# Linear attention and an ELU feed-forward on one core: K and V of four batches on all 128 rows, one chunk moved up, the last copy split

## The chip, the cores and the metric

The kernel runs on one core of one Trainium2 chip. The metric is device time in microseconds of that core, as the median of several executions of the whole program. The engines named below are PE (TensorE, matmuls, with its weight loads), DVE (VectorE), ACT (ScalarE), POOL (GpSimd, which here also issues the loads) and SP (SyncE, which issues transposing transfers and stores). PSUM is the memory that PE writes its sums to.

## The reference

Eight batches with eight heads of 576 rows and 64 columns go through linear attention, a norm per head, and a feed-forward with an ELU between two matrices of 512 x 2048 and 2048 x 512.

```python
kv = np.einsum('bhsd,bhse->bhde', k, v)
out = np.einsum('bhsd,bhde->bhse', q, kv)
rms = np.sqrt(np.mean(out * out, axis=-1, keepdims=True) + 1e-06)
x = out / rms * g_norm            # then heads side by side: 4608 tokens of 512
h = x @ w_in
g = np.where(h > 0.0, h, np.exp(np.minimum(h, 0.0)) - 1.0)
return g @ w_out
```

## The kernel before

A tile is 512 tokens, so there are nine tiles (`NT`) over eight batches. One tile is cut from rows that lie 64 to a group: a head's 576 rows are 64 groups of nine consecutive rows (`RK` = 9), and a matmul takes one row of each group.

**K and V.** `load` (L88) lays a batch of K or V into a tile `[128, 4, 9, 64]`: partition and index m together run through the heads, so that two heads lie on the two halves of the partitions, and each partition holds nine rows of a head in one piece of 2304 bytes of float32, which the DMA turns to bfloat16. `kv_mm` (L151) makes K^T V of the eight heads: for each of nine rows, two partition halves `s`, and two column halves `l`, for two values of `u`, one matmul of 64 rows x 64 columns with 64 elements; 72 in a batch. The four quarters of the array are taken in turn. The sums go to `kv_sb` (L268 by ACT, for batches 2 to 7).

**Order.** The order of work is written out by hand (a manual schedule); only waits and buffers are placed by the framework. Each engine works through its own list in order. Batch 0 is made in four chunks of two heads, L577 to L652: `chunk_kv` (K^T V), `chunk_kv_out` (its copy by DVE), `chunk_y` (q times it), `chunk_square` (ACT), `mean_mm` (the mean over a head by a matmul with a constant matrix), a logarithm and an exponential on ACT for one over the root, `chunk_scale` (DVE), and `early` (the products with `w_in` for the first three pairs of blocks, chunk by chunk). `idle` (L523) issues matmuls with zeros that fill waiting time. After that PE alternates products of the first matrix (`mm1`, L390, 32 groups of four for a tile), of the second (`mm2`, L399) and pieces of the next tile's attention. From tile 2 on that is `window` (L753), in which `kv` of batch T + 1 stands behind the first pair of blocks of tile T.

**Loads.** They are issued by POOL in the order of the program. For batches 2 to 7 `fetch_ahead` (L92) issues q, K and V; `cast_q` (L98) rearranges q on POOL after that; `turn_q` (L328) turns it by DMA on SP; and `after_turn` (L336) holds POOL until q is turned, before the next batch is fetched. The tiles of K and V come from a pool with three buffers each. Software DMAs share eight semaphores in turn, so a DMA also waits for the one eight before it.

**End.** The last tile's last 128 tokens are made in two halves of 256 columns by `last_columns` (L434): 16 matmuls, then a copy from PSUM (ACT for the first half, DVE for the second, L448), then `last_store` (L423), one store on ACT's queue and one on SP's.

Of the kernel before, what the change touches and what calls it, by code (L numbers as in the profile page):

```python
# [9 lines left out]
BF16 = mybir.dt.bfloat16  # L10
# [6 lines left out]
def kernel(  # L17
# [13 lines left out]
    nc = tc.nc  # L31
    P = 128

    B, H, S, D = q.shape
    DM = H * D
    DF = moe_w_in.shape[1]
    RK = S // 64
    J = 4
# [3 lines left out]
    NT = B + 1  # L42
    V, A, Q = nc.vector, nc.scalar, nc.gpsimd
# [3 lines left out]
    qkvp = ctx.enter_context(tc.tile_pool(name="qkvp", bufs=3))  # L47
# [27 lines left out]
    def slot_of(T, n):  # L75
        return divmod(8 * T + n, RK)

    bf, raw = {}, {}
    src_of = {"q": q, "k": k, "v": v}

    def fetch(name, b, u=None):

        if (name, b) not in bf:
            bf[name, b] = qkvp.tile([P, 4, RK, D], BF16, name=f"{name}_bf", tag=name)
        ms = slice(0, 4) if u is None else slice(u, 4, 2)
        load(bf[name, b][:, ms], name, b, ms)

# [4 lines left out]
    def fetch_ahead(b):  # L92
        raw[b] = stage.tile([P, 4, RK, D], FP32, name="st_q", tag="q")
        load(raw[b], "q", b)
        for name in "kv":
            fetch(name, b)

    def cast_q(b):  # L98

# [8 lines left out]
    def copy_on(eng, out_, in_):  # L108
        if eng is nc.scalar:
            nc.scalar.copy(out_, in_)  # L110
        else:
            eng.tensor_copy(out=out_, in_=in_)  # L112
# [16 lines left out]
    def single(tag, name):  # L129
        pool = ps_x if tag == "x" else ps_m2  # L130
        return pool.tile([P, 512], FP32, name=name, tag=tag)

    def pair(tag, name):
        if tag in ("x", "m", "mx"):
            return [single(t, name) for t in (tag + tag)[:2]]
        return ps_m1.tile([P, 2, 512], FP32, name=name, tag=tag)
# [14 lines left out]
    def kv_mm(b, kv_ps, u, ls=range(2)):  # L151
        for j in range(RK):
            for s in range(2):
                rows = slice(s * 64, s * 64 + 64)
                for l in ls:
                    nc.tensor.matmul(  # L156
                        kv_ps[s][l * 64 : l * 64 + 64, u * 64 : u * 64 + 64],
                        lhsT=bf["k", b][rows, 2 * l + u, j, :],
                        rhs=bf["v", b][rows, 2 * l + u, j, :],
                        start=(j == 0),  # L160
                        stop=(j == RK - 1),
                    )

    def kv_out(b, kv_ps, u, engs):
        for s in range(2):
# [92 lines left out]
    def attention(T):  # L258

        st = {}  # L260

        def kv():
            if T == B:
                return
            kv_ps = at_tile()
            for u in range(2):
                kv_mm(T, [kv_ps[:, s, :] for s in range(2)], u)
            nc.scalar.copy(  # L268
                kv_sb[:, T], kv_ps[:, :, 0:P].rearrange("p s (u e) -> p u s e", u=2)
            )  # L270

        def se(h):
            def product():
                st["se", h] = at_tile()
                se_mm(T, h, st["se", h])
                sq = attp.tile([P, 2, DM], BF16, name="sq", tag="sq")
                nc.scalar.activation(sq, st["se", h], AF.Square)  # L277
                st["sq", h] = sq

            def sums():  # L280
                ss = attp.tile([P, 2 * H], FP32, name="ss", tag="ss")
                st["ss", h] = ss
                nc.vector.reduce_sum(  # L283
                    out=ss,
                    in_=st.pop(("sq", h)).rearrange("p l (m e) -> p (l m) e", e=D),
                    axis=AX.X,
                )

            def inv():
                ss = st["ss", h]  # L290
                nc.scalar.activation(ss, ss, AF.Ln, bias=eps_col, scale=1.0 / D)
                nc.scalar.activation(ss, ss, AF.Exp, scale=-0.5)  # L292

            def scale():
                if h == 0:
                    st["xs"] = attp.tile([P, J, DM], BF16, name="xs", tag="xs")
                    x_tile(T)
                se_ps, ss = st.pop(("se", h)), st.pop(("ss", h))
                nc.vector.tensor_tensor(  # L299
                    out=st["xs"][:, 2 * h : 2 * h + 2, :].rearrange("p i (l m e) -> p l i m e", l=2, e=D),  # L300
                    in0=se_ps.rearrange("p l (i m e) -> p l i m e", i=2, e=D),
                    in1=ss.rearrange("p (l i m) -> p l i m", l=2, i=2).unsqueeze(4).to_broadcast([P, 2, 2, 4, D]),
                    op=ALU.mult,
                )
                for i in (2 * h, 2 * h + 1):
                    nc.sync.dma_start_transpose(
                        out=xT[T][:, :, i * P : i * P + P], in_=st["xs"][:, i, :]
                    )

            def gain():  # L310
                cols = slice(2 * h * P, 2 * h * P + 2 * P)
                nc.vector.tensor_scalar(  # L312
                    out=xT[T][:, :, cols],
                    in0=xT[T][:, :, cols],
                    scalar1=g_col,
                    scalar2=None,
                    op0=ALU.mult,
                )

            return product, sums, inv, scale, gain  # L320

        pieces = {"kv": kv}
        for h in range(2):
            for name, piece in zip(("se", "sum", "inv", "mul", "gain"), se(h)):
                pieces[f"{name}{h}"] = piece
        return pieces
# [96 lines left out]
    def last_store(j, o, cols):  # L423
        rows = out_dram.rearrange("(b p j) f -> b p j f", b=B, j=RK)
        for h, eng in enumerate((nc.scalar, nc.sync)):
            b, jj = slot_of(NT - 1, 2 * j + h)
            eng.dma_start(out=rows[b][:, jj, cols], in_=o[h * 64 : h * 64 + 64])
# [5 lines left out]

    def last_columns():  # L434

        for n, eng in enumerate((A, V)):
            cols = slice(n * 256, n * 256 + 256)
            ps = single("m", "o_ps")[:, 0:256]
            for f in range(FC):
                nc.tensor.matmul(  # L440
                    ps,
                    lhsT=gT[NT - 1][:, f, (J - 1) * P : J * P],
                    rhs=w_out_sb[:, f, cols],
                    start=(f == 0),
                    stop=(f == FC - 1),
                )
            o = outp.tile([P, 2, DM], FP32, name="o_sb", tag="o")[:, 0, 0:256]
            copy_on(eng, o, ps)  # L448
            last_store(J - 1, o, cols)

    def mm2_half(T, i):
        mm2(T, i // 2, 8 * (i % 2), 8 * (i % 2) + 8)
# [20 lines left out]

    low, high = slice(0, 5), slice(5, 9)
    for name in "qkv":
        bf[name, 0] = qkvp.tile([P, 4, RK, D], BF16, name=f"{name}_bf", tag=name)
    first = {"q": first_load("q", (0, 2)), "k": first_load("k", (0,)), "v": first_load("v", (0,))}
    g_row = const.tile([1, 2, 64], FP32, name="g_row")
    one = const.tile([1, 1], FP32, name="one")
# [43 lines left out]
    def idle(n, ps):  # L523
        for _ in range(n):
            nc.tensor.matmul(ps, lhsT=zeros[:, 0:P], rhs=zeros, start=True, stop=True)  # L525
# [10 lines left out]
    def chunk_kv(kv_ps, c):  # L536
        kv_mm(0, [kv_ps[:, s, :] for s in range(2)], c % 2, (c // 2,))

    def chunk_kv_out(kv_ps, c, eng):
        rows, cols = slice(c // 2 * 64, c // 2 * 64 + 64), slice(c % 2 * 64, c % 2 * 64 + 64)  # L540
        copy_on(eng, kv_sb[rows, 0, c % 2], kv_ps[rows, :, cols])

    y_ps, sq0 = {}, {}

    def chunk_y(c, ps):
        y_ps[c] = ps
        y_mm(0, c % 2, {c // 2: ps}, (c // 2,))

    def chunk_square(c):
        sq0[c] = attp.tile([P, G], BF16, name="sq", tag="sq")  # L550
        nc.scalar.activation(sq0[c], y_ps[c], AF.Square)

    def chunk_scale(c, r, cols=slice(0, 512)):
        scale_t(0, y_ps[c][:, cols], r[:, cols], c, cols)
# [55 lines left out]
    inv_t(r[:, 1, :], mean)  # L610
    kv_ps = pair("B", "kv_ps")
    h_ps = [pair("A", "h_ps")]
    idle(2, h_ps[0][:, 0, :])
    chunk_kv(kv_ps, 1)
    chunk_kv_out(kv_ps, 1, V)
    idle(1, h_ps[0][:, 0, :])
    chunk_y(1, single("m", "y_ps"))
    chunk_square(1)
    chunk_scale(0, r[:, 0, :])
    idle(1, h_ps[0][:, 0, :])  # L620
    chunk_kv(kv_ps, 3)
    chunk_kv_out(kv_ps, 3, V)
    chunk_scale(2, r[:, 1, :])
    mean = single("m", "mean")
    mean_mm(sq0[1], mean)
    r = r_tile()
    nc.scalar.activation(r[:, 0, :], mean, AF.Ln, bias=eps_col)
    y3 = single("x", "y_ps")
    h_ps += [None, [single("x", "h_ps"), None]]
    chunk_y(3, y3)  # L630
    chunk_square(3)
    h_ps[1] = pair("B", "h_ps")
    early([(0, 0), (0, 1), (1, 0), (1, 1), (2, 0)], 0)
    for n in range(2):
        cols = slice(n * 256, n * 256 + 256)
        nc.scalar.activation(r[:, 0, cols], r[:, 0, cols], AF.Exp, scale=-0.5)
# [195 lines left out]
```

## Time and profile before

| what | value |
|---|---|
| median of 3 runs | 285.79 us (285.79 to 286.7) |
| profiled execution, in all | 285.81 us |
| its span, first to last instruction | 284.0 us |
| PE busy | 277.8 us (98%), 2124 matmuls |
| DVE, ACT, POOL busy | 164.7, 141.3, 49.1 us |
| second matrix (L403) | 560 matmuls, 129.7 us |
| first matrix (L382) | 560 matmuls, 128.0 us |
| K^T V (L156) | 576 matmuls of 64 x 64, 64 elements |
| K load, V load, batches 2 to 7 | 6 each, 576 KB, 10.4 and 12.4 us to landing |
| q load, batches 2 to 7 | 6, 1152 KB, 7.9 us to landing |

Matmuls are pipelined; the busy time of a group is the time that it covers, and the mean of one (about 0.38 us for 512 columns) is longer than the step from one to the next (0.216 us). The chain of work that ended last is followed back from the last instruction, at each step to what released it. Times in the chain and in the timelines count from the start of the span.

### The profile page before, as it was taken

To read this page: it belongs to the slowest core of one execution; us is meant where nothing else is said; L and a number is where in the kernel's file an instruction comes from. 1 tells how busy PE (TensorE), PEld (TensorE's weight loads), DVE (VectorE), ACT (ScalarE), POOL (GpSimd) and SP (SyncE) were. 2 spreads that over 40 slices of the span, in tenths; PEclk is the share of its full clock that TensorE was granted. 3 is DMA by queue.
4 is the path that set the end of the run, shared out by engine and by line. 5 is a ranking of instruction groups with operands and counts; after the bars stand their busy time and mean duration, and the time that the engine had idled before them with its cause. 6 is when DMAs were issued, how large, how long until landed. Compare 5 with 4: busy or idle time off the path is not lost.

```text
span 284.0 us, 5154 instructions
## 1 busy us (share of the span) xinstructions
PE 277.8 (98%) x2124; PEld 129.5 (46%) x2124; DVE 164.7 (58%) x222; ACT 141.3 (50%) x209; POOL 49.1 (17%) x89
## 2 busy tenths in 40 slices
PE   8899999999999999999999999999999999999994
PEld 3444444444644444444444444444444444444443
DVE  2449632977487657655785478537872787344500
ACT  4678359595567355434542555245533553333320
POOL 8743303313340033033003300000000000000000
PEclk9999999999999999999999999999999999999999
DMA  7999999999895979589538961602150235020222
GB/s 210 194 204 206 207 260 240 193 300 141 191 274 77 161 210 227 71 197 258 146 28 181 262 156 38 160 19 74 39 111 0 74 39 111 0 76 0 74 74 75
DMA packets 50571, 39.46 MB, mean 139 GB/s; under 512 B 30964, under 2 KB 44020, under 8 KB 50548
## 3 DMA queue, kind: packets, MB, share of 16 engines
q0 software_dynamic: 15008, 21.30, 37.5%
q1 hardware_dynamic: 35136, 17.31, 28.9%
q10 hardware_dynamic: 404, 0.53, 0.5%
q8 instruction: 16, 0.26, 0.4%
q14 instruction: 7, 0.06, 0.1%
HBM read 36.70 MB, written 9.44 MB: 162 GB/s over the span
## 4 chain that ended last, share of the span: by engine, by line
PE 96%; DVE 1%; DMA 1%; ACT 0%; issue 0%; DVEq 0%
PE o_ps L403 43%; PE h_ps L382 42%; PE at L250 2%; PE kv_ps L525 2%; PE h_ps L569 2%; PE at L156 1%; PE qt_ps L174 1%; PE kv_ps L156 1%; PE y_ps L189 1%; PE mean L199 1%; DMA out_dram<-o_sb 1%; PE o_ps L440 1%; DVE gT L366 0%; ACT elu_e L350 0%; DVE kv_sb L112 0%; PE h_ps L525 0%
## 5 line engine op out<-in xcount | busy, mean ns | idle before, releaser
L403 PE MATMUL o_ps<-w_out_sb,gT 128*128 128x512 bf16 x560 | 129.7, 379 | 0.0
L382 PE MATMUL h_ps<-xT,w_in_sb 128*128 128x512 bf16 (+1 forms) x560 | 128.0, 376 | 0.1
L350 ACT ACTIVATE elu_e<-h_ps 128x1024 bf16<-128x1024 f32 (+1 forms) x79 | 74.0, 952 | 89.1 <-PE h_ps L382 86.4
L403 PEld LDWEIGHTS <-gT 128*128 128x128 bf16 x560 | 54.4, 98 | 65.8 <-issue 0.9
L382 PEld LDWEIGHTS <-w_in_sb 128*128 128x128 bf16 x560 | 53.2, 98 | 61.3 <-issue 0.4
L366 DVE TENSOR_TENSOR gT<-elu_e,h_ps 128x1024 bf16<-128x1024 bf16 (+1 forms) x67 | 77.2, 1157 | 6.6
L362 DVE TENSOR_SCALAR elu_e<-elu_e 128x1024 bf16<-128x1024 bf16 x72 | 31.3, 435 | 65.3 <-ACT elu_e L350 65.2
L419 ACT COPY o_sb<-o_ps 128x512 f32<-128x512 f32 x32 | 18.3, 587 | 21.1 <-PE o_ps L403 21.1
L103 POOL CAST q_bf<-st_q 128x384 bf16<-128x384 f32 x36 | 17.7, 535 | 39.4 <-DMA st_q<-in_q_dram 34.3
L283 DVE TENSOR_REDUCE ss<-sq 128x16 f32<-128x1024 bf16 x14 | 17.1, 1219 | 6.6 <-ACT sq L277 6.6
L299 DVE TENSOR_TENSOR xs<-at,ss 128x1024 bf16<-128x1024 f32 x14 | 17.1, 1218 | 1.9 <-ACT ss L292 1.9
L277 ACT ACTIVATE sq<-at 128x1024 bf16<-128x1024 f32 x14 | 14.4, 1029 | 0.0
L212 DVE SCALAR_TENSOR_TENSOR xT<-y_ps,g_col,rT 128x512 bf16<-128x512 f32 (+1 forms) x10 | 6.2, 640 | 9.8 <-ACT rT L209 7.9
L339 POOL COPY gate<-qT 1x16 bf16<-1x16 bf16 x5 | 1.1, 229 | 58.5 <-DMA qT<-q_bf 58.5
L355 ACT ACTIVATE elu_h<-h_ps 128x1024 bf16<-128x1024 f32 (+1 forms) x12 | 9.3, 817 | 0.0
L156 PEld LDWEIGHTS <-k_bf 64*64 64x64 bf16 x576 | 6.3, 107 | 5.0 <-issue 4.6
L90 POOL DMA_DIRECT2D k_bf<-in_k_dram x11 | 7.9, 722 | 3.1 <-DMA w_in_sb<-in_moe_w_in_dram 2.3
L90 POOL DMA_DIRECT2D v_bf<-in_v_dram x11 | 7.7, 699 | 4.2 <-DMA w_in_sb<-in_moe_w_in_dram 2.1
L312 DVE TENSOR_SCALAR xT<-xT,g_col 128x1024 bf16<-128x1024 bf16 x14 | 6.7, 480 | 1.8 <-DMA xT<-xs 1.8
L250 PEld LDWEIGHTS <-qT 64*128 64x128 bf16 (+1 forms) x248 | 4.3, 97 | 6.1 <-issue 5.9
L112 DVE COPY o_sb<-o_ps 128x256 f32<-128x256 f32 x1 | 0.4, 425 | 11.5 <-DMA out_dram<-o_sb 11.5
L366 DVE TENSOR_TENSOR gT<-elu_e,elu_h 128x1024 bf16<-128x1024 bf16 x9 | 6.4, 716 | 0.8
(57 smaller groups left out, 102.4 us busy)
## 6 DMA issues: line engine op xcount, KB each, us to landing
st_q<-in_q_dram POOLq DMA_DIRECT2D x6, 1152.0 KB, 7.9
out_dram<-o_sb SPq DMA_DIRECT2D x24, 256.0 KB, 3.3
k_bf<-in_k_dram POOLq DMA_DIRECT2D x6, 576.0 KB, 10.4
v_bf<-in_v_dram POOLq DMA_DIRECT2D x6, 576.0 KB, 12.4
out_dram<-o_sb SPq DMA_DIRECT2D x19, 128.0 KB, 2.4
w_out_sb<-in_moe_w_out_dram POOLq DMA_DIRECT2D x4, 512.0 KB, 14.9
w_in_sb<-in_moe_w_in_dram POOLq DMA_DIRECT2D x2, 512.0 KB, 11.1
q_bf<-in_q_dram POOLq DMA_DIRECT2D x3, 288.0 KB, 13.4
```

Source lines behind the costliest of these rows:

```text
L90: eng.dma_start(out=dst.rearrange("p m j d -> p m (j d)"), in_=in_[:, ms, :])
L103: nc.gpsimd.tensor_copy(out=bf["q", b][:, u, js], in_=raw[b][:, u::2, js, :].rearrange("p l j d -> p j l d"),)
L156: nc.tensor.matmul(kv_ps[s][l * 64 : l * 64 + 64, u * 64 : u * 64 + 64], lhsT=bf["k", b][rows, 2 * l + u, j, :], rhs=bf["v", b][rows, 2 * ...
L277: nc.scalar.activation(sq, st["se", h], AF.Square)
L283: nc.vector.reduce_sum(out=ss, in_=st.pop(("sq", h)).rearrange("p l (m e) -> p (l m) e", e=D), axis=AX.X,)
L299: nc.vector.tensor_tensor(out=st["xs"][:, 2 * h : 2 * h + 2, :].rearrange("p i (l m e) -> p l i m e", l=2, e=D), in0=se_ps.rearrange("p l ...
L350: nc.scalar.activation(e[:, lo:hi, :], h, AF.Exp)
L362: nc.vector.tensor_scalar(out=e, in0=e, scalar1=1.0, scalar2=1.0, op0=ALU.min, op1=ALU.subtract)
L366: nc.vector.tensor_tensor(out=gT[T][:, 2 * i + lo : 2 * i + hi, :], in0=e[:, lo:hi, :], in1=h, op=ALU.add if relu else ALU.max,)
L382: nc.tensor.matmul((ps[a] if isinstance(ps, list) else ps[:, a, :])[:, cols], lhsT=w_in_sb[:, c, f * P : f * P + P], rhs=xT[T][:, c, cols] ...
L403: nc.tensor.matmul(o_ps[T, j], lhsT=gT[T][:, f, j * P : j * P + P], rhs=w_out_sb[:, f, :], start=(f == 0), stop=(f == FC - 1),)
L419: nc.scalar.copy(o_sb[T, half][:, j % 2, :], o_ps[T, j])
```

## The change

It has three parts.

1. For batches 4 to 7 (`TALL`), K and V are loaded by `fetch_tall` in place of `fetch`. A head lies on all 128 partitions: the lower 64 hold five consecutive rows each (320 of a head's 576), the upper 64 hold four (256) and a fifth that a POOL memset fills with zeros. That makes two memsets and four DMAs (64 partitions each) per batch where there were two DMAs. `kv_mm_tall` makes a head's K^T V by five matmuls over 128 rows, with the two column halves `l` in turn; 40 in a batch. The tiles of q, K and V have one size for all batches (`qkv_tile`), which is larger than before.
2. In batch 0, K^T V of chunk 1 comes ahead of the two filler matmuls, one filler is gone, K^T V of chunk 3 and y of chunk 3 come before the mean of chunk 1, and the scaling of chunk 0 comes before the copy of K^T V of chunk 3. The first two `early` products come before the mean of chunk 1, and the square of chunk 3 before its logarithm.
3. The copy of the last 256 columns is split: ACT copies the first 128, DVE the other 128. Each half is stored for all 128 tokens by one DMA, ACT's half on ACT's queue and DVE's on SP's, with 512 bytes per token.

```diff
+    TALL, RT = 4, 5
+    def fetch_tall(name, b):
+        t = qkvp.tile([P, H * RT * D], BF16, name=f"{name}_bf", tag=name)
+        bf[name, b] = t.rearrange("p (h j d) -> p h j d", h=H, j=RT)
+        rows = src_of[name][b]
+        nc.gpsimd.memset(bf[name, b][64:P, :, RT - 1, :], 0.0)
+        for lo, n, r0 in ((0, RT, 0), (64, RT - 1, 64 * RT)):
+            nc.gpsimd.dma_start(
+                out=bf[name, b][lo : lo + 64, :, 0:n, :].rearrange("p h j d -> p h (j d)"),
+                in_=rows[:, r0 : r0 + 64 * n, :].rearrange("h (p j) d -> p h (j d)", p=64),
+            )
...
+    def kv_mm_tall(b, kv_ps):
+        for u in range(2):
+            for s in range(2):
+                for j in range(RT):
+                    for l in range(2):
+                        nc.tensor.matmul(
+                            kv_ps[s][l * 64 : l * 64 + 64, u * 64 : u * 64 + 64],
+                            lhsT=bf["k", b][:, 4 * l + 2 * u + s, j, :],
+                            rhs=bf["v", b][:, 4 * l + 2 * u + s, j, :],
+                            start=(j == 0),
+                            stop=(j == RT - 1),
+                        )
...
-            copy_on(eng, o, ps)
-            last_store(J - 1, o, cols)
+            if n == 0:
+                nc.scalar.copy(o, ps)
+                last_store(J - 1, o, slice(0, 256))
+                continue
...
+            for copy_eng, store_eng, lo in ((A, nc.scalar, 0), (V, nc.sync, 128)):
+                copy_on(copy_eng, o[:, lo : lo + 128], ps[:, lo : lo + 128])
+                store_eng.dma_start(
+                    out=rows[:, :, 256 + lo : 384 + lo],
+                    in_=o[:, lo : lo + 128],
+                )
...
     h_ps = [pair("A", "h_ps")]
-    idle(2, h_ps[0][:, 0, :])
     chunk_kv(kv_ps, 1)
     chunk_kv_out(kv_ps, 1, V)
-    idle(1, h_ps[0][:, 0, :])
+    idle(2, h_ps[0][:, 0, :])
+    chunk_scale(0, r[:, 0, :])
+    chunk_kv(kv_ps, 3)
+    chunk_kv_out(kv_ps, 3, V)
     chunk_y(1, single("m", "y_ps"))
     chunk_square(1)
-    chunk_scale(0, r[:, 0, :])
     idle(1, h_ps[0][:, 0, :])
-    chunk_kv(kv_ps, 3)
-    chunk_kv_out(kv_ps, 3, V)
+    y3 = single("x", "y_ps")
+    h_ps += [None, [single("x", "h_ps"), None]]
+    chunk_y(3, y3)
+    chunk_square(3)
     chunk_scale(2, r[:, 1, :])
+    h_ps[1] = pair("B", "h_ps")
+    early([(0, 0), (0, 1)], 0)
     mean = single("m", "mean")
     mean_mm(sq0[1], mean)
     r = r_tile()
     nc.scalar.activation(r[:, 0, :], mean, AF.Ln, bias=eps_col)
-    y3 = single("x", "y_ps")
-    h_ps += [None, [single("x", "h_ps"), None]]
-    chunk_y(3, y3)
-    chunk_square(3)
-    h_ps[1] = pair("B", "h_ps")
-    early([(0, 0), (0, 1), (1, 0), (1, 1), (2, 0)], 0)
+    early([(1, 0), (1, 1), (2, 0)], 0)
```

## The prediction

> **What bounds the kernel now.** I read the page first, then busy time by stretch, then the chain in order of time, then the timelines at the places the change touches. Busy time by stretch (us, then each engine's busy time and count, granted clock, DMA share, GB/s):
>
> ```profile
> 0.00:21.90 21.90, 19.88 (x168) 8.74 (x169) 8.89 (x24) 13.24 (x22) 14.39 (x27) 1.00 1.07 203
> 21.90:276.40 254.50, 254.49 (x1926) 117.91 (x1926) 155.34 (x198) 127.14 (x188) 34.70 (x62) 1.00 0.65 135
> 276.40:284.00 7.60, 3.44 (x32) 2.83 (x29) 0.42 (x1) 0.94 (x2) 0.00 (x0) 0.92 0.27 70
> ```
>
> TensorE (PE, first number) is busy for 254.49 of the middle 254.50 us. There, only fewer or cheaper PE steps help. In the first 21.9 us PE has 2.0 us of gaps, and after its last matmul comes a tail. The chain that ended last, in order of time (start, length, what):
>
> ```profile
> 11.27 0.48 PE h_ps L525 x2
> 11.75 0.42 PE kv_ps L156 x18
> 12.17 0.02 issue
> 12.19 0.29 DVE kv_sb L112
> 12.49 0.04 issue
> 12.53 0.41 PE y_ps L189 x2
> 12.93 0.32 PE h_ps L525
> 13.26 0.42 PE kv_ps L156 x18
> 13.68 0.02 issue
> 13.70 0.31 DVE kv_sb L112
> 14.00 0.04 issue
> 14.05 0.40 PE y_ps L189 x2
> 14.45 1.62 PE h_ps L569 x7
> ...
> 99.16 0.71 PE at L156 x72
> ...
> 278.53 1.77 DMA out_dram<-o_sb
> 280.31 0.41 DVE o_sb L112
> ```
>
> See two holes near 12.2 and 13.7, where PE waits for VectorE (DVE) to copy the K^T V sum it has just made; the 0.71 us of a K^T V block of 72 matmuls; and the last copy, after which only its store remains.
>
> **What the Trainium skill says.** "TensorEngine Tiling (Array Packing)", Tiling Modes, lets 128x64 run as two independent tiles and 64x64 as four, and says a change of mode drains the array. The trace agrees: 64x64 matmuls start in bursts of four, 3 ns apart, one burst per 31.7 ns, and the step from a 128x128 matmul into such a block is 0.31 us against 0.216 us. "TensorE: Matmul & The Clock Gate", LDWEIGHTS, makes a weight load cost columns/1.2 ns whatever the rows: 53 ns for 64 columns. The trace does not show that as a bound: four such loads fit in each 31.7 ns. "PSUM — Partial Sum Buffer", PSUM bank collisions, has ScalarE and VectorE reads of one bank and partition collide, with the back end ordering them. "DMA: Bandwidth & Descriptors", Specifications, puts line rate at 512 B and above; here 512 descriptors that write 512 B each (`w_in` blocks 6 and 7) landed 1.03 us after the piece ahead of them, twice as many bytes in 1024 B writes took 2.53 us, so the trace agrees.
>
> **Part 1, tall K and V (batches 4 to 7).** A block of 72 becomes 40: 20 pairs, each over all 128 rows and both column halves. Today the first to last start of 72 take 0.58 us (18 bursts at 31.7 ns, the first longer). No 128-row, 64-column, 64-element matmul is in the trace, so I bound the pair's period:
> - Below: 64 columns at the streaming rate of a 128x512 matmul (512 in 216 ns) are 27 ns; 20 pairs with the same longer first one, 0.56 us: 0.02 us less per block.
> - Nearest rows: the query product (L250, 64x128 tiles, 64 elements, two row halves) starts a pair every 30.4 ns; turned q (L174, 128x64 tiles, 128 elements, two column halves) every 56 ns, which is 53 ns of streaming plus 3.
> - Above: if a weight load of 128 rows needs twice the 8 ns that a 64-row one has, 40 x 16.6 ns + 0.05 = 0.71 us: 0.13 us more.
>
> I take 31 ns: about 0.61 us, 0.025 us more, so **+0.1 us over four blocks** (-0.1 to +0.5). Halving the matmul count saves nothing, since bursts of four were already full: 72/4 = 18 periods become 40/2 = 20. The steps into and out of the mode stay (0.31 and 0.13 us).
>
> Loads: K and V of one batch are 4 DMAs with 2048 descriptors, where they were 2 with 1024; pieces of 1280 and 1024 B for 2304 B, 640 and 512 B written. At line rate they take as long as before. They cost POOL per batch two more DMA issues (0.75 us each) and two memsets of 512 bf16 (the 128-element one is 0.20 us; I take 0.5 us each), 2.5 us. They stand between the q load and the six casts of q. For batch 4 POOL is free at 76.5 us and its casts start at 81.6, with the load: cover of 5 us. For batch 5, 103.5 and 107.2: cover of 3.7 us. Without that cover, casts, turning of q and then the gate for the next fetch move by the excess. V of batch 4 lands near 87.7 us for a block at 99.1, of batch 5 near 115 for 128.4. The eight DMA lanes now wrap after 1.6 batches, but the transfer each issue waits for is a batch old. Cost 0; if loads took twice as long, still 0.
>
> **Part 2, chunk 3 of batch 0 moved up.** By rows of the timeline. The mean of chunk 2 starts at 10.88 us in both.
> - K^T V of chunk 1 no longer waits behind two filler matmuls: 10.88 + 0.31 = 11.19, last start 11.47. Its K and V landed at 9.7 and 10.4. DVE is busy with qT until 11.68, copies 11.70 to 11.99, then scales chunk 0 (0.73 us) to 12.65.
> - Fillers 11.59 and 11.81. K^T V of chunk 3: 12.11 to 12.58 (V landed 11.8). Its copy now queues behind the scaling: 12.65 to 12.95; y of chunk 3 waits for it. y of chunk 1 12.40, filler 12.73, y of chunk 3 13.05. First product with `w_in` 13.39, for 14.38; `w_in` chunk 0 lands at 13.2, so this is also near its floor.
> - Not all is kept. The mean of chunk 1 now comes after two of these products, 13.83 for 13.62, and its logarithm starts 0.21 us later on ACT. ACT's square of chunk 3 now precedes that logarithm: scaling of chunk 1 ends at 16.29 for 16.42. The first product with chunk 1 would be due at 15.99 and waits to 16.35 (for 16.77). From there five products, two of the sixth bank, and chunk 3 at 17.86 and 18.08 (chunk 3 scaled by 17.65, its weights landed 17.34). Today they start at 18.42 and 18.63.
>
> The elu chain at 19.05 and everything behind it move up by **0.55 us** (0.35 to 0.75). What is late next is fixed by DMA: `w_out` slice 1 lands at 32.80 and is first used at 33.45, so 32.90 after the move; 0.1 us is left. Slice 3: 42.24 for 43.03.
>
> **Part 3, last columns.** PE's last matmul ends at 279.85. Today DVE copies 256 columns at 280.29 to 280.71, both queues store at 280.74, the last store lands at 282.93; 1.1 us of closing barrier follows. In the built program the ACT half waits for PE, but DVE's half waits for ACT's copy, not for PE: the two do not overlap. ACT started 0.03 us after PE for the first 256 columns, so 279.88; 512 columns take 0.585 and 256 take 0.372, so 128 take 0.27: 280.14. DVE 280.18, 128 columns by the line through 1 (0.16) and 256 columns (0.425) 0.29: 280.47. SP's store at 280.49, 1.94 us as today plus up to 0.2 for twice the descriptors (128 of 512 B): 282.5. Gain **0.4 us** (0.1 to 0.5). Part of it is that DVE today starts 0.44 us after PE although its other waits ended earlier; if that lag is DVE's own and returns, 0.1 is left.
>
> **Sum.** Profiled execution: span 284.0, 285.81 us in all, within 0.02 of the median 285.79. -0.55 + 0.1 - 0.4 = -0.85: 284.95 us.
>
> **Rivals.**
> - *The early gain is swallowed.* `w_out` slice 1 and later q turned for batch 3 (lands 76.3 for a use at 77.35) don't move with PE, or chunk 1's scaling comes later still. For it: DMA is full until 33 us. Against: 0.1 us left by my count. Then 0.25 of the 0.55 stays: 285.25. The same time if DVE's lag returns in the tail.
> - *Slower: column halves don't overlap in the tall blocks.* 40 x 30 ns = 1.2 us for 0.58, +2.5 us over four blocks, less 0.95: 287.35. For it: the skill's 53 ns per load would give a pair 53 ns (+1.9 us). Against: turned q runs such pairs 4 ns apart. It decides once a tall matmul takes over 26 ns (0.45 us more a block, against 0.95 gained and 0.86 of tolerance).
> - *Part 1 does what its count suggests.* 40/72 of 0.58 us is 0.32: -1.0 more, 283.9. Against: bursts of four are bound by streaming.
>
> **How the numbers follow.** A measurement of this kernel tells no less than 0.3% (0.86 us). Forecast 0.62, swallowed 0.20, slower 0.10, count rival 0.08. The forecast lies on the edge of 0.3% (284.93), so half of it (0.31) counts as faster; with the count rival 0.4 in round numbers. Within 0.3%: the other half and the swallowed gain, 0.5. Slower: 0.1. Range 284.2 to 286.2: it takes in the swallowed gain and the upper price of part 1, and leaves out the slower rival and most of the count rival.
>
> **What would show it.** Blocks of 40 with pairs every 29 to 33 ns; first `w_in` product at 13.4 and first elu at 18.5; `w_out` matmuls at 32.9 without a hole; ACT's and DVE's last copies one after the other, DVE done near 280.5 less the early gain. Wrong if a tall block takes over 0.75 us, if PE has holes at 32.9 or 76.8, or if the last store lands less than 0.5 us earlier than today.

## The result and the profile after

The changed kernel is slower: 287.78 us (287.57 to 288.25) against 285.87 us for the kernel before on the same chip, a ratio of 1.0063 with a 95% interval of 1.0040 to 1.0086. A second comparison on another occasion gave 288.47 against 285.95 us, 1.0092 (1.0073 to 1.0110). The forecast was 284.95 us, its range ended at 286.2.

The profiled execution of the changed kernel took 288.25 us in all, with a span of 286.5 us where the kernel before had 284.0. First, busy time by stretch of the changed kernel, cut at the same places (stretch, length, then PE, PE's weight loads, DVE, ACT and POOL with their counts, granted clock, DMA share, GB/s):

```profile
0.00:21.90 21.90, 18.93 (x170) 8.51 (x171) 9.39 (x25) 13.89 (x23) 14.24 (x27) 1.00 1.07 201
21.90:276.40 254.50, 254.26 (x1795) 117.61 (x1794) 155.45 (x197) 126.60 (x185) 43.87 (x79) 1.00 0.68 136
276.40:286.50 10.10, 3.81 (x34) 3.07 (x32) 0.29 (x1) 1.22 (x3) 0.00 (x0) 0.87 0.20 53
```

PE is as full in the middle as before (254.26 for 254.49 us). The last stretch is 2.5 us longer, but PE's part of it only 0.37 us. The chain that ended last, in order of time:

```profile
2.67 6.33 DMA q_bf<-in_q_dram
...
9.29 8.48 DMA w_in_sb<-in_moe_w_in_dram
...
18.05 14.98 DMA w_out_sb<-in_moe_w_out_dram
33.02 0.04 issue
33.07 1.89 PE o_ps L444 x8
...
73.21 0.84 PE at L179 x72
...
99.36 0.75 PE at L193 x40
...
280.23 0.02 issue
280.25 0.27 ACT o_sb L133
280.52 0.02 issue
280.55 0.29 DVE o_sb L135
```

Four readings. From 2.67 to 33.02 us it goes through loads (q, `w_in`, `w_out`), where the chain of before went through the first K^T V copies; so the early work no longer sets the start alone. A tall block (L193) takes 0.75 us, which is just the limit that the prediction named, where one of 72 took 0.71. ACT's and DVE's last copies stand one after the other, as the prediction had them. And DVE is done at 280.84, 0.13 us later than before: nothing in the chain accounts for the remaining 2 us. They come after the last copy.

The trace splits the change of span (+2.42 us) so:

| | before | after | difference |
|---|---|---|---|
| last matmul ends | 279.85 | 280.21 | +0.36 |
| from there to the last landing of a store | 3.08 | 5.22 | +2.14 |
| closing barrier | 1.11 | 1.03 | -0.08 |
| span | 284.04 | 286.46 | +2.42 |

The DMA view of the stretch after the last issues shows the store itself. First the kernel before (281.5 to 284 us), where the two last stores are all that moves:

```profile
DMA packets 160, 0.13 MB, mean 52 GB/s; under 512 B 32, under 2 KB 160, under 8 KB 160
q1 hardware_dynamic: 80, 0.07, 11.1%
q10 hardware_dynamic: 80, 0.07, 10.4%
```

Then the changed kernel (281.5 to 286.4 us), the same bytes:

```profile
DMA packets 260, 0.13 MB, mean 27 GB/s; under 512 B 4, under 2 KB 260, under 8 KB 260
q10 hardware_dynamic: 130, 0.07, 4.9%
q1 hardware_dynamic: 130, 0.07, 4.5%
```

The packets under 512 B are the writes that report completion. Before there are 32, 16 for each store; after there are 4, two for each. So each store of the changed kernel ran on two DMA engines, and the trace has both stores on the same two. Each store has 128 pieces of 512 B, so each engine has 64 of either store and takes about 26 ns for one: ACT's store is through from 281.76 to 283.93, SP's at 285.11. Before, both stores were through in 0.73 us, 281.86 to 282.59. Landing follows at 285.43 for 282.93. A busy share by stretch says it in another way (281 to 286 us of the changed kernel, two of its five rows):

```profile
283.00:284.00 1.00, 0.00 (x0) 0.00 (x0) 0.00 (x0) 0.00 (x0) 0.00 (x0) 0.96 0.14 41
284.00:285.00 1.00, 0.00 (x0) 0.00 (x0) 0.00 (x0) 0.00 (x0) 0.00 (x0) 0.50 0.14 44
```

All five engines are idle, and 0.14 of the DMA capacity is in use: 2 of 16 engines would be 0.125.

### The profile page after: what moved, and what is told of

Same layout as the page of the kernel before. It is cut to its first block, busy times and chain, and to the rows that moved or that the text cites. A ratio compares the mean times of both kernels' runs of the same rounds, so it can differ in the third digit from the quotient of the medians.

```text
span 286.5 us, 4913 instructions
## 1 busy us (share of the span) xinstructions
PE 277.0 (97%) x1995; PEld 129.2 (45%) x1995; DVE 165.1 (58%) x222; ACT 141.7 (49%) x210; POOL 58.1 (20%) x105
## 4 chain that ended last, share of the span: by engine, by line
PE 86%; DMA 10%; POOL 1%; issue 0%; DVE 0%; ACT 0%; POOLq 0%
PE o_ps L444 41%; PE h_ps L423 39%; DMA w_out_sb<-in_moe_w_out_dram 5%; DMA w_in_sb<-in_moe_w_in_dram 3%; DMA q_bf<-in_q_dram 2%; PE at L287 2%; PE o_ps L481 1%; PE at L193 1%; PE at L179 1%; PE mean L236 0%; POOL k_bf L110 0%; PE y_ps L226 0%; PE qt_ps L211 0%; POOL v_bf L110 0%; PE kv_ps L179 0%
## 5 line engine op out<-in xcount | busy, mean ns | idle before, releaser
L135 DVE COPY qT<-qt_ps 128x1024 bf16<-128x1024 bf16 (+1 forms) x8 | 3.3, 454 | 5.0 <-PE qt_ps L211 5.0
L620 PE MATMUL h_ps<-xT,w_in_sb 128*128 128x512 bf16 x24 | 5.8, 380 | 0.3 <-DVE xT L249 0.2
L287 PE MATMUL at<-kv_sb,qT 64*128 64x64 bf16 (+1 forms) x248 | 6.1, 193 | 0.0
```

Source lines behind the costliest of these rows:

```text
L287: nc.tensor.matmul(se_ps[lo:hi, l, (4 * i + m) * 64 : (4 * i + m) * 64 + 64], lhsT=qT[b][l * 64 : l * 64 + 64, s, u, j : j + n, :], rhs=kv ...
```

## The experiments

**Theory and rivals.** Theory: the loss is in part 3 alone, and there in the shape of the store, not in the split copy. Rival A: parts 1 and 2 lose in the middle. Rival B: the loss is in part 3, but comes from pieces of 512 B for 1024 B. Rival C: it comes from the outer dimension of the store, which is two groups of tokens, whatever the pieces.

| run | median us | before | ratio (95%) | last matmul | span |
|---|---|---|---|---|---|
| changed kernel | 287.78 | 285.87 | 1.0063 (1.0040 to 1.0086) | 280.21 | 286.46 |
| part 3 undone | 285.30 | 285.73 | 0.9992 (0.9981 to 1.0002) | 279.65 | 283.47 |
| part 3 alone | 287.86 | 285.73 | 1.0071 (1.0047 to 1.0095) | 279.75 | 286.07 |
| split copy, four stores | 285.55 | 285.73 | 0.9998 (0.9984 to 1.0012) | 279.71 | 283.69 |
| whole copy, one store | 288.27 | 285.73 | 1.0090 (1.0070 to 1.0109) | 279.79 | 286.64 |
| part 1 alone | 285.95 | 285.95 | 1.0001 (0.9993 to 1.0009) | 279.98 | 284.14 |
| part 2 alone | 285.09 | 285.95 | 0.9970 (0.9959 to 0.9981) | 279.56 | 283.40 |
| part 2, last copy by ACT | 285.29 | 285.95 | 0.9987 (0.9977 to 0.9997) | 279.56 | 283.51 |
| changed kernel, again | 288.47 | 285.95 | 1.0092 (1.0073 to 1.0110) | 280.65 | 286.92 |
| part 1 without batch 5 | 286.10 | 285.98 | 1.0006 (0.9993 to 1.0018) | 279.80 | 283.97 |
| part 2 alone, again | 285.54 | 285.98 | 0.9985 (0.9973 to 0.9996) | 279.48 | 283.33 |

### Part 3 undone, and part 3 alone

The changed kernel with the old end:

```diff
-            for copy_eng, store_eng, lo in ((A, nc.scalar, 0), (V, nc.sync, 128)):
-                copy_on(copy_eng, o[:, lo : lo + 128], ps[:, lo : lo + 128])
-                store_eng.dma_start(
...
+            copy_on(eng, o, ps)
+            last_store(J - 1, o, cols)
```

> The changed kernel with part 3 undone: the last 256 columns copied by DVE[...], as before. Theory (the two last stores are slow because their descriptors go one after another): the tail after the last matmul returns from 6.2 to 4.2 us, and the time falls from 287.8 by 2.0 to 285.8. Rival (the time went to PE, not to the stores): no more than 0.5 us comes back, 287.3 or more.

The reverse, the kernel before with the new end:

```diff
-            copy_on(eng, o, ps)
-            last_store(J - 1, o, cols)
+            for copy_eng, store_eng, lo in ((A, nc.scalar, 0), (V, nc.sync, 128)):
+                copy_on(copy_eng, o[:, lo : lo + 128], ps[:, lo : lo + 128])
+                store_eng.dma_start(
...
```

> The kernel before with part 3 alone. Theory: 2.0 us slower than before, 287.8, with the last store landing about 4.5 us after its issue. Rival (the slow store comes from something that parts 1 and 2 set up): 285.4, 0.4 us faster as predicted.

Measured: 285.30 us without part 3, 287.86 us with it alone. The two runs are each other's mirror: part 3 costs 2.1 us by itself (287.86 - 285.73) and 2.3 us on top of the others (1.91 in the first comparison and the 0.43 that the others gain). From the last matmul to the end of the span it is 4.19 us before, 3.82 with part 3 undone, 6.25 in the changed kernel and 6.32 with part 3 alone. Rival A falls as the cause of the slower time. Part 3 alone came as expected (ACT's store lands 3.7 us after its issue, SP's 4.6). Part 3 undone came back further than expected, 3.82 us for 4.2, because DVE's late start of the last copy was gone as well; why is seen below with part 2.

### Which property of the store

The split copies stay, but each half is stored by two DMAs of 64 tokens, still in pieces of 512 B:

```diff
-                store_eng.dma_start(
-                    out=rows[:, :, 256 + lo : 384 + lo],
-                    in_=o[:, lo : lo + 128],
-                )
+                for h in range(2):
+                    b, jj = slot_of(NT - 1, 2 * J - 2 + h)
+                    store_eng.dma_start(
+                        out=rows[b][:, jj, 256 + lo : 384 + lo],
+                        in_=o[h * 64 : h * 64 + 64, lo : lo + 128],
+                    )
```

> The changed kernel, with copies split as in part 3, but each half stored by two DMAs of 64 tokens x 128 columns (512 B pieces still, outer dimension 64 and not 2). Theory (it is the outer dimension of 2 that puts all descriptors of a store on two DMA engines): a store lands about 2 us after its issue, and the time is 285.4 to 285.8. Rival (512 B pieces are slow wherever they go): the last landing stays over 3.5 us after issue, 287 or more.

And the kernel before, with DVE's whole copy of 256 columns stored by one DMA on SP over both groups of tokens, in pieces of 1024 B:

```diff
-            last_store(J - 1, o, cols)
+            if n == 0:
+                last_store(J - 1, o, cols)
+                continue
+            b, jj = slot_of(NT - 1, 2 * J - 2)
+            rows = out_dram.rearrange("(b p j) f -> b j p f", b=B, j=RK)[b, jj : jj + 2]
+            nc.sync.dma_start(out=rows[:, :, cols], in_=o)
```

> The kernel before, with the last copy whole on DVE, and its 256 columns stored by one DMA on SP for both groups of 64 tokens (outer dimension 2, pieces of 1024 B). Theory (outer dimension): slow too, 128 descriptors on two engines, landing 4 to 5 us after issue, 287.7 or more. Rival (512 B pieces): one store of 1024 B pieces lands in about 2.3 us, 286.0 or less.

The DMA view after the last issues, four stores in pieces of 512 B (281.1 to 283.6 us):

```profile
DMA packets 320, 0.13 MB, mean 53 GB/s; under 512 B 64, under 2 KB 320, under 8 KB 320
```

and one store in pieces of 1024 B (281.5 to 286.5 us):

```profile
DMA packets 130, 0.13 MB, mean 26 GB/s; under 512 B 2, under 2 KB 130, under 8 KB 130
```

Four stores over 64 tokens report 64 times, 16 each, and each lands 1.8 to 1.9 us after its issue (the pieces of 512 B are no slower). One store over [2, 64, 256] reports twice and lands 4.8 us after its issue, with pieces of 1024 B at 51 ns a piece and engine. So rival B falls and rival C stands: what matters is that the store's outermost dimension is 2. In time, 0.9998 against 1.0090. The four stores also have another number of DMAs, but two stores were fast in the kernel before and slow with part 3 alone, so that isn't it. One DMA over all 128 tokens with 64 as its outermost dimension was not tried.

The Trainium skill states this. "DMA: Bandwidth & Descriptors", section "Why a DMA increments its semaphore by 16 and not by 1", has it that a DMA runs on k of 16 engines, the largest k up to 16 that divides the slowest dimension that isn't 1 of both access patterns (here 2 in DRAM and the 128 partitions), and that for a DMA of SP or ACT only these k count the semaphore up, while the sequencer that issued it writes the other 16 - k at once. "Rules for kernel authors" adds that an outermost dimension below 16 confines the whole DMA. The trace agrees: 2 reports and 0.14 of the DMA capacity for an outermost 2, 16 reports for an outermost 64. The semaphore's records, too, show three steps for such a store (281.53, 284.20 and 284.24 for ACT's) where a store of before shows 16.

With these four stores the split copy gains nothing. The two copies end 0.63 us after PE's last matmul; the one of 256 columns ends 0.52 us after it with part 3 undone, and 0.87 in the kernel before, where DVE starts late. Each queue also issues two stores, the second 0.51 us after the first. The last landing is at 282.79, against 282.39 with part 3 undone. What the split would give with one fast store per queue was not measured.

### Part 1 alone

The kernel before with `qkv_tile`, `fetch_tall` and `kv_mm_tall` and their calls, batch 0 and the end as they were:

```diff
+            if b >= TALL:
+                fetch_tall(name, b)
...
+            if T >= TALL:
+                kv_mm_tall(T, halves)
```

> The kernel before with part 1 alone (tall K and V of batches 4 to 7). Theory (a block of 40 takes 0.626 us from first to last start, as the trace of the changed kernel has it, for 0.582): +0.045 us each, +0.2 in all, 285.9 beside 285.75. Rival (fewer matmuls are worth something, or the new loads or memsets cost more): below 285.7 or above 286.3.

Measured: 1.0001 (0.9993 to 1.0009); span 284.14 for 284.04 us. By the records of matmul starts, a block of 40 takes 0.626 us from first to last, where 72 took 0.582, in this run and in all others but for two blocks of 72 in the first profile of the changed kernel: +0.044 us, +0.18 us for four blocks. 40 matmuls for 72, no time saved.

The trace shows a second effect, while PE works on tile 3. The rows of DVE's multiplication by the gain for the next tile, which waits for x to be turned by DMA, first in the kernel before, then with part 1 alone, then in the second execution of the changed kernel (start, length, and in brackets idle time and its cause):

```profile
116.85 0.48 DVE L312 TENSOR_SCALAR xT<-xT,g_col 128x1024 bf16<-128x1024 bf16 x1
```

```profile
117.50 0.49 DVE L353 TENSOR_SCALAR xT<-xT,g_col 128x1024 bf16<-128x1024 bf16 x1 [0.74 <-DMA xT<-xs]
```

```profile
118.17 0.49 DVE L353 TENSOR_SCALAR xT<-xT,g_col 128x1024 bf16<-128x1024 bf16 x1 [1.28 <-DMA xT<-xs]
```

Two of the four transposing transfers of this x are issued at 109.5 and 110.7 us, while the tall K and V of batch 5 are on their way (from 102 to 115 us, to 118 in the second execution); the other two come at 116.8 and 118.0. DVE's next product for PE is pushed back, and PE has a hole of 0.17 us at 119.31 with part 1 alone, of 0.71 us in the second execution of the changed kernel, and none in its first, where DVE waited 0.35 us. The second execution's chain goes through it:

```profile
110.84 7.31 DMA xT<-xs
...
118.17 0.49 DVE xT L353
...
119.10 1.23 DVE gT L407
...
120.37 1.89 PE h_ps L423 x8
```

### Part 1 without batch 5

To see whether that load is the cause, batch 5 was loaded and multiplied in the old way:

```diff
-            if b >= TALL:
+            if b >= TALL and b != 5:
```

> Part 1 alone, but batch 5 is fetched and multiplied in the old way; the tall form stays for batches 4, 6 and 7. If the tall load of batch 5 is what made the transposing transfers of x for the next tile late, VectorE's multiplication by the gain in that tile starts near 116.6 to 116.9 us again, as in the kernel before, instead of 117.5 or later, waits for no transfer, and TensorE has no gap near 119.3. If the delay is chance or belongs to the tall load of batch 4, it stays. Time by either: 285.7 to 286.1 us; three tall blocks cost 0.04 us each.

The same row of DVE:

```profile
116.72 0.48 DVE L353 TENSOR_SCALAR xT<-xT,g_col 128x1024 bf16<-128x1024 bf16 x1
```

The wait and the hole are gone, and batch 5's block comes 29.37 us after batch 4's as before (29.34), where it was 29.54 with the tall load. The other profiles agree: the second of the two transfers lands 6.07 to 7.31 us after its issue in the five with the tall load of batch 5, and 4.65 to 5.71 in the seven without. So the tall load of batch 5 makes x late. DVE waits 0 to 1.28 us for it, and PE was held in two of the five profiles (0.17 and 0.71 us). In the time of the whole it is below what can be told (1.0006, 0.9993 to 1.0018).

### Part 2 alone, and a variant

The kernel before with the changed order of batch 0, and nothing else:

```diff
+    chunk_scale(0, r[:, 0, :])
+    chunk_kv(kv_ps, 3)
+    chunk_kv_out(kv_ps, 3, V)
     chunk_y(1, single("m", "y_ps"))
...
+    early([(0, 0), (0, 1)], 0)
     mean = single("m", "mean")
```

> The kernel before with part 2 alone (chunks 1 and 3 of batch 0 moved). Theory: the K^T V block of batch 3 starts at 72.7 for 73.1 and the rest follows, 0.4 us faster: 285.35. Rival (the gain is swallowed between 33 and 73 us, by a late slice of the second matrix or by the turned x of tile 2): the block of batch 3 starts within 0.1 us of 73.1, 285.7.

Measured twice: 0.9970 (0.9959 to 0.9981) and 0.9985 (0.9973 to 0.9996).

> Part 2 alone, measured once more. If its gain is real, the ratio to before is again near 0.997 (285.1 us), with the last matmul about 0.3 us earlier than before. If the first comparison was luck with load landings, the ratio is 0.999 to 1.001.

This is the version that beats the kernel before, by 0.9 and 0.4 us. The second ratio lies between its two expectations, but its interval leaves out 1. The block of batch 3 starts at 72.81 and 72.73 us for 73.08, so 0.27 and 0.35 us of the 0.4 expected arrive there, and the rival (swallowed before 73 us) falls.

Of the first span's 0.64 us, only 0.29 are PE's (279.56 for 279.85); the other 0.35 is DVE's start of the last copy: 0.10 us after PE's end instead of 0.44. The last copy in the kernel before, then with part 2 alone:

```profile
280.29 0.42 DVE L112 COPY o_sb<-o_ps 128x256 f32<-128x256 f32 x1 [11.45 <-DMA out_dram<-o_sb]
```

```profile
279.66 0.42 DVE L112 COPY o_sb<-o_ps 128x256 f32<-128x256 f32 x1 [11.10 <-PE o_ps L440]
```

The store that the first row names did not hold it. The trace's records of DVE's own waits show that the wait for PE ended at 279.89, and that DVE then paused for 0.40 us. A pause of 0.40 to 0.45 us stands ahead of the same place in DVE's list, its 320th recorded instruction, in eleven of the twelve profiles (with part 3 alone the wait for ACT's copy covers that place). Part 2 gives DVE one more wait, so with it the pause falls between two waits while PE still works (275.96 to 276.38 us) and costs nothing. So more than half of this span's gain comes from where a pause happens to fall, and not from the earlier chunk.

What limits the first share is seen in the changed stretch. From the second mean of batch 0 to the first elu it takes 8.17 us in all five profiles without part 2 (10.88 to 19.05 in the kernel before). With part 2 it takes 7.63 us in three profiles and 8.04 to 8.35 in four. The two ends of the stretch in the kernel before, then in the changed kernel with part 3 undone:

```profile
10.88 0.39 PE L199 MATMUL mean<-sq,ones 128*128 128x512 bf16 x1
...
19.05 1.94 ACT L350 ACTIVATE elu_e<-h_ps 128x1024 bf16<-128x1024 f32 x2 [1.29 <-PE h_ps L569]
```

```profile
11.05 0.39 PE L236 MATMUL mean<-sq,ones 128*128 128x512 bf16 x1
...
18.68 1.94 ACT L391 ACTIVATE elu_e<-h_ps 128x1024 bf16<-128x1024 f32 x2 [1.47 <-PE h_ps L610]
```

PE's rows inside it in one of each kind with part 2, first part 2 alone (8.27 us), then the changed kernel with part 3 undone (7.63 us):

```profile
13.27 0.60 PE L569 MATMUL h_ps<-xT,w_in_sb 128*128 128x512 bf16 x2
...
16.62 2.55 PE L569 MATMUL h_ps<-xT,w_in_sb 128*128 128x512 bf16 x11 [0.59 <-DMA w_in_sb<-in_moe_w_in_dram]
```

```profile
13.58 0.60 PE L610 MATMUL h_ps<-xT,w_in_sb 128*128 128x512 bf16 x2
...
16.54 2.53 PE L610 MATMUL h_ps<-xT,w_in_sb 128*128 128x512 bf16 x11 [0.19 <-DVE xT L249]
```

The first waits for a load, the second for DVE. In seven profiles `w_in` chunk 0 lands between 13.12 and 13.40 us. Chunk 1 lands at 15.1 to 15.5 in four of them and at 16.57 to 16.77 in three, where one of its sixteen parts came 1.4 to 1.5 us after the others; in the kernel before it was needed at 16.77, so a late part was covered, and with part 2 at 16.4. The first elu stands at 18.54 to 18.97 with part 2, and at 18.84 to 19.05 without. The wall is the arrival of `w_in`, which does not move with PE. The three profiles with 7.63 us are those whose second mean itself came late, at 11.03 to 11.07 us for 10.48 to 10.73 in the other four, so that their loads had more time. In the first profile of the changed kernel no part of the first two chunks was late, but chunk 0 landed at 13.40 and held the first product to 13.45: 8.06 us.

With the last 256 columns copied by ACT instead of DVE on top of part 2:

```diff
-        for n, eng in enumerate((A, V)):
+        for n, eng in enumerate((A, A)):
```

> The kernel before with part 2, and with the last copy of 256 columns on ACT in place of DVE (stores as before). ACT starts 0.03 us after PE and takes 0.37 us; DVE took 0.43 us and started 0.1 to 0.46 us after PE. Theory: 0.4 us from part 2 and 0.1 to 0.45 from the copy, 285.0 to 285.25. Rival (ACT's store issue or a wait behind it holds it up): as part 2 alone.

Measured 0.9987 (0.9977 to 0.9997), no better than part 2 alone. ACT starts 0.04 us after PE, and the last store lands at 282.20 instead of 282.31; but the span ends 1.31 us after that, for 1.09. DVE's pause now falls there, from 282.71 to 283.16 us, in the closing barrier. Neither the expected gain nor its rival (ACT's issue of the store) tells what happened.

### The changed kernel once more

The same kernel, with no edit, beside the runs of parts 1 and 2 alone:

> The changed kernel once more. In its first profile the K^T V blocks of batches 2 and 3 took 0.11 us more than before and PE waited 0.24 us for the turned x of tile 2; the same instructions without part 3 did neither. Theory (that was of one execution): blocks of 0.58 us, last matmul 0.2 us earlier than before, and a tail of 6.2 us from the last matmul to the end; 287.3 to 287.8. Rival (the change does it): the same holes again, last matmul 0.35 us later than before.

Measured 288.47 us, 1.0092 (1.0073 to 1.0110), with the last matmul 0.80 us later than before: neither the expectation nor its rival. The end is the same (6.27 us after the last matmul). PE is 0.44 us later than in the first profile. Of PE's time, the second profile had gained only 0.08 us before the hole of 0.71 us at 119.4, and the four tall blocks cost another 0.18. The first profile was 0.39 us ahead at the block of batch 2 (53.70 for 54.09 us) and lost that elsewhere: K^T V of batches 2 and 3 took 0.69 and 0.70 us for 0.58, PE waited 0.34 us at 70.7 for x of tile 2, and the tall blocks took their 0.18. The losses ahead of the tall blocks did not come back in the second profile or in those of the other kernels with parts 1 and 2; they belong to that execution, and their cause stays open.

## Why the prediction was wrong

**Part 3, SP's store: the step that failed.** The prediction had "SP's store at 280.49, 1.94 us as today plus up to 0.2 for twice the descriptors". It is the term of 2.1 us that measured 4.6 us. The store was costed by its bytes and its number of pieces; its access pattern [2, 64, 128] was not looked at. As a store over 64 tokens has 16 engines and one over 2 x 64 has two, both stores queue there: ACT's takes 3.7 us, SP's, behind it, 4.6 us. Part 3 measured +2.1 us for -0.4, and this alone turns the sign. The prediction named late landing as a sign of being wrong, but gave no rival with it.

**Part 3, the copies: right.** ACT 0.27 us, DVE 0.29 us, one after the other, DVE's copy done 0.59 us after ACT's begins; as costed. The lag of DVE (0.44 us) was DVE's own, as the prediction feared: a pause at a fixed place of its list. It did not return with part 3, but part 2 takes it off the path too, so on top of part 2 the split copies end no earlier than the single one (0.63 us after the last matmul for 0.52).

**Part 1, the pair's period: right in kind, a little short in size.** 31 ns was taken and 31.7 measured, the period that a burst of four has today: +0.044 us per block for +0.025, +0.18 for +0.1. Both rivals on it fall: halves of the array do overlap (1.2 us per block would have been needed), and the count is worth nothing.

**Part 1, loads at no cost: wrong in part.** The cover was sought for the work behind the loads (casts, turning of q, the blocks that use K and V) and that held. Not asked was what shares the DMA engines with a tall load: two transposing transfers of x, issued in the middle of batch 5's. The second lands late, and PE lost 0 to 0.71 us by execution.

**Part 2: the walk right, what is kept less.** The order of waits came out as described, and where the loads had time the stretch from the second mean to the first elu shrank by 0.54 us (8.17 less 7.63) for 0.55. But chunk 0 of `w_in` was taken as "near its floor" and chunk 1 not at all; they are the floor. About 0.2 us is kept at the first elu (mean of seven profiles 18.73, of the five without part 2 18.95), 0.29 at the end of part 2 alone. The first profile of the changed kernel did show the named signs, a first product at 13.45 and a first elu at 18.54, but with a second mean 0.40 us earlier than in the walk, so that was luck in part. What is kept is near the rival "the early gain is swallowed", one group of loads earlier than it said. `w_out` slice 1, its own suspect, did hold PE in one profile (landing at 33.02, first use at 33.07), by a load that came 0.2 us later than before.

**The sum.** With part 3 undone the time is 285.30 us, inside the range and 0.35 above the forecast, but that agreement is largely luck. It has no gain from part 3 in it, its interval (0.9981 to 1.0002) includes no change, and of its span's gain of 0.57 us only 0.20 are PE's; 0.37 come from DVE's pause falling elsewhere. The rival "slower" named nearly the right time (287.35) for a mechanism that did not happen.

## What to carry to other kernels

Before two stores from SP or ACT are merged into one, read the outermost dimension: where it dropped from 64 to 2 here, the store dropped from 16 DMA engines to 2, and at the end of a kernel all of that is on the path (2.1 us here for two stores of 64 KB). Where matmuls on quarters of the array already start in full bursts, fewer matmuls over more rows saved no time (both start every 31.7 ns). Work that is moved up meets loads that don't move with it: look up the landing of every piece that the moved work uses, and how far it varies, before counting the whole step as gained. And look at where a gain stands in the span: a copy that starts earlier by itself can hide in the total as if the change had earned it.

## What the runs showed of the hardware

- A store over [2, 64, 128] of float32 lands 3.7 us after its issue, 4.6 us behind another such; over [2, 64, 256] 4.8 us; stores over 64 tokens 1.8 to 2.2 us. A piece of 512 B takes 26 ns on its DMA engine, one of 1024 B 51 ns; two engines give some 40 GB/s.
- DVE pauses for 0.40 to 0.45 us ahead of the same place in its list, the 320th recorded instruction, in eleven of twelve profiles. The last copy of 256 columns starts 0.44 to 0.46 us after PE's last matmul in the four where the pause falls there, and 0.09 or 0.10 us in three where it falls earlier. In these seven an instruction fetch of 8 KB begins 0.5 to 0.7 us after the pause (near 280.9 or near 277 us). Whether the two belong together was not tried, and the cause of the pause is open.
- One of the sixteen parts of a `w_in` load came 1.3 to 1.5 us after the other fifteen, in one execution at chunk 1, in another of the same program at chunk 3. What delays it is open.
- The second transposing transfer of x landed 6.07 to 7.31 us after its issue beside a load with 512 B and 640 B writes (five profiles), and 4.65 to 5.71 us beside the old form of that load (seven). That the delay comes from sharing DMA engines is argued, not measured by itself.
